# Keys prepared one pair earlier, and the division of x shared by two engines

## The chip, the cores and the metric

The kernel runs on one core of a Trainium2 chip. The metric is device time in microseconds, from one launch to its end. A core has five engines that matter here, each working through its own list of instructions in order: TensorE (PE: matrix products and transposes), VectorE (DVE), ScalarE (ACT), GpSimd (POOL), and SyncE (SP), which issues most of the DMA transfers. They wait for each other by semaphores only.

## The reference

The inputs pass through three stages. First attention without a score matrix, for 8 batches of 8 heads, 576 tokens and 64 dimensions:

```
q_s = exp(q - max over the 64 dimensions), divided by its sum (+1e-9)
k_s = exp(k - max over the 576 tokens),    divided by its sum (+1e-9)
kv  = k_s^T v            (64x64 for each head)
x   = q_s kv             (4608 tokens of 512 numbers, heads side by side)
```

Then a mixture of 8 experts: a gate picks for each token the expert with the largest logit (`x @ w_gate` plus a bias of the token's modality), and the token gets `gate * relu(x @ w1[e]) @ w2[e]`. Then a dense stage for all tokens: `a = x @ w1`, `b = x @ w2`, `out = (a * b) @ w3 @ w_out`.

## The kernel before, in words

**Order of the work.** The steps are not issued in the order of the source. Each is handed to `Plan.add` with its engine ("P" PE, "V" DVE, "S" ACT, "G" POOL, "D" a DMA on SP, "X" bookkeeping), an estimated cost in us, the keys that it reads and writes, and a `pri` that shifts its rank. `Plan.order` plays the list through with these costs: of the engines' next possible steps it takes the earliest, and among the steps that an engine could start within 0.02 us the one with the lowest rank. What comes out is the fixed order of instructions on each engine. The costs and the rank therefore decide only the order; the real times are the chip's. One such plan holds all of attention and the first part of the experts; it ends at a branch (L772), behind which a second plan holds the rest.

**Attention.** The 8 batches are taken as four pairs, `c` = 0 to 3, with `z = c % 2` choosing one of two buffers for keys, values and queries. For each pair there are these pieces:

- `load` (L246) issues the DMAs of q, k or v.
- `keys(c)` (L276): DVE takes maxima over the token blocks (L285 to L288), PE turns the result into PSUM bank 5 (L294), DVE finishes the maximum (L297), PE spreads it back to rows in bank 5 (L302), ACT copies it out (L305). Then, for four groups of heads, POOL subtracts it from the keys (L310; for the first pair DVE does) and ACT takes the exponential in place (L311).
- `kvs(c)` (L313): for each group of heads ACT copies the values beside a column of ones (L322), and PE multiplies keys by values in banks 4 and 5, 72 products a group (L329). DVE divides (L336 to L338), and a turn, a product with the gate weights and copies follow (L342 to L353). The result `bd` is what queries are multiplied with.
- `queries(n)` (L355): three tiles of queries at once get their row maximum subtracted on DVE (L364, L365). There are three such steps for a pair.
- `attend(c, j)` (L367), for nine tiles of 128 tokens, `j` = 0 to 8: PE turns the queries (L379), ACT takes the exponential (L382), PE multiplies with `bd` into a pair of PSUM banks `px` (L392), four heads of 73 columns in each bank: 64 of x, the sum, 8 of the gate. ACT copies the sums plus 1e-9 (L402) and the gate columns (L403), DVE takes the reciprocal (L404) and multiplies both banks by it into the x tile `xt` (L405). Two tiles together are stored to DRAM (L409).
- `route(c)` (L421) gives the pair's tokens their places in the experts' lists: some fifteen small DVE steps in a chain, PE products in bank 4 (L443, L445), and nine POOL scatters of 128 rows each (L416, `scatter`).

The main loop (L729 on) calls for pair `c`: the load of the keys of pair `c + 2`, `keys(c + 1)`, `route(c - 1)`, the nine `attend` with `queries` among them, the load of the queries, `kvs(c + 1)`, the load of the values. At `c = 2` it also makes the table of the first experts' work (`early_table`, L533), a chain of some thirty DVE instructions on single rows.

**Experts.** `slot` (L573) handles 512 or 256 tokens of one expert: SP reads the table (L571) and loads the order (L594) and the weights (L600), POOL gathers the tokens (L605), ACT scales them (L609). ACT and DVE split weights and tokens into a high and a low part (L586, L588, L629, L630), and PE multiplies (L642, L662). The first three slots draw on the tokens of pairs 0 and 1 alone, but their buffers take the place of attention's: `to_experts_a` (keys and values of even pairs) and `to_experts_b` (the rest, after all of attention; key `Mb`). The dense stage (L794 on) is nearly all PE.

Of the kernel before, what the change touches and what calls it, by code (L numbers as in the profile page):

```python
# [11 lines left out]
AF = mybir.ActivationFunctionType  # L12
ALU = mybir.AluOpType
# [5 lines left out]
B, H, S, D = 8, 8, 576, 64  # L19
NTOK = B * S  # L20
E = 8
NT = 9
# [94 lines left out]
def K(*a):  # L117
    return a


def vt_(n):
    return 0.065 + n * 0.00125
# [17 lines left out]
def body(tc, q, k, v, mod, wgate, mbias, w1, w2, m1, m2, w3, wo, out):  # L140
    nc = tc.nc
    V, G, SC, PE, SP = nc.vector, nc.gpsimd, nc.scalar, nc.tensor, nc.sync
# [133 lines left out]
    def keys(c):  # L276
# [18 lines left out]

        P.add("P", 0.9, over_partitions, r=[K("mx", z)], w=[K("bk", 5)])
        P.add("V", vt_(512), lambda: V.tensor_reduce(x_, bk.rearrange("p (c t) -> p c t", c=8), axis=AX.X, op=ALU.max), r=[K("bk", 5)], w=[K("cm", z)])  # L297
# [15 lines left out]
    def kvs(c):  # L313
# [6 lines left out]
        for g in range(4):  # L320
# [9 lines left out]

            P.add("P", 1.4, mm, r=[K("k", z, g), K("vp", g % 2)], w=[K("bk", 4), K("bk", 5)])
        for y in range(2):
# [34 lines left out]
    def attend(c, j):  # L367
# [12 lines left out]

        P.add("P", 0.9, tr, r=[K("qs", y)], w=[K("bk", qb)])
        P.add("S", ps_(512), lambda: SC.activation(T, pt, AF.Exp), r=[K("bk", qb)], w=[K("qT", n)])  # L382
# [10 lines left out]

        P.add("P", 0.8, mm, r=[K("qT", n)] + [K(x_, 2 * z + y) for x_ in ("bd", "bdg") for y in range(2)], w=pk)
        xb = (j // 2 + 5 * c) % 5
# [5 lines left out]
        by_bank = lambda t: t.rearrange("p (b g) e -> p b g e", b=2)  # L401
        P.add("S", 0.22, lambda: SC.activation(by_bank(r_.unsqueeze(2)), pv[:, :, :, 64:65], AF.Identity, bias=eps), r=pk, w=[qk])  # L402
        P.add("S", 0.22, lambda: SC.copy(by_bank(l_), pv[:, :, :, 65:73]), r=pk, w=[lk])  # L403
        P.add("V", 0.2, lambda: V.reciprocal(r_, r_), w=[qk])  # L404
        P.add("V", vt_(512), lambda: V.tensor_tensor(xdst, pv[:, :, :, 0:64], by_bank(r_.unsqueeze(2)).to_broadcast([128, 2, 4, 64]), op=ALU.mult), r=pk + [qk, lk], w=[rkey])  # L405
        if j % 2 or j == NT - 1:
            js = slice(j - j % 2, j + 1)
            dst = x_dram[128 * NT * c : 128 * NT * c + 128 * NT].rearrange("(p j) f -> p j f", j=NT)[:, js]
            P.add("D", 0.7 * (j % 2 + 1), lambda: SP.dma_start(dst, xt[xb][:, 0 : j % 2 + 1]), r=[K("xt", xb, i) for i in range(j % 2 + 1)], w=[K("x", c, j // 2)])  # L409

# [10 lines left out]
    def route(c):  # L421
# [34 lines left out]
        for t in range(NT):  # L456
            P.add("G", (1.04, 0.1), lambda t=t: scatter(pi[:, t : t + 1], tid[:, c, t]), r=[K("pi", z), K("gate", c), "order"], w=[K("scat", NT * c + t)], pri=-40)

# [268 lines left out]
    kvs(0)  # L727
    biases()
    for c in range(4):  # L729
        load("k", c + 2)  # L730
        keys(c + 1)
        if c:
            route(c - 1)
        if 2 * c == BEARLY:
            early_table()
        if c == 3:
            fa_keys = [k_ for k_ in P.last if isinstance(k_, tuple) and k_[0] in ("k", "v") and k_[1] == 0] + ["mods", K("mods", 0), K("mods", 1), K("bias", 1), "bs", "bsb", "mod", "modf", "zer"]
            P.add("X", 0.0, to_experts_a, w=fa_keys + ["Ma"])
        for j in range(NT):
            attend(c, j)  # L740
            if j % 3 == 2:
                queries(3 * c + j // 3 + 2)
        load("q", c + 2)
        kvs(c + 1)
        load("v", c + 2)
    fb_keys = [k_ for k_ in P.last if isinstance(k_, tuple) and (k_[0] in ("q", "qs", "qx", "qT", "bd", "bdg", "mx", "kr", "cm", "rk", "kT", "vp") or k_[0] in ("k", "v") and k_[1] == 1)]
# [222 lines left out]
```

## Time and profile before

| | us |
|---|---|
| median of 3 runs | 1305.44 (1302.25 to 1308.61) |
| the profiled execution | 1308.98, span 1307.3 |
| PE busy | 1210.3 (93%) |
| DVE busy | 642.1 (49%) |
| ACT busy | 450.9 (34%) |
| POOL busy | 282.6 (22%) |

The span is the time between the first and the last instruction of the profiled execution; 1.7 us of its time lie outside it. Busy shares are means over very different stages, so they have to be read for each stretch by itself. Times in the traces count from the span's start. "Idle before, releaser" tells how long an engine had stood idle before an instruction and which instruction let it go on; "issue" is waiting for which the profile shows no cause.

### The profile page before, as it was taken

What the parts mean: (1) busy time and instruction counts of PE and PEld (TensorE: products, weight loads), DVE (VectorE), ACT (ScalarE), POOL (GpSimd) and SP (SyncE); (2) the same over time, 40 slices, a digit from 0 to 9 for tenths busy, and PEclk for the clock granted to TensorE, in tenths of its full rate; (3) what the DMA queues carried; (4) which work ended last, traced back from release to release, by engine and by line L of the source; (5) the groups of instructions that cost most, each with busy time, mean ns of one, the idle gap of its engine ahead of it and who ended that gap; (6) DMA issues with size and microseconds to landing.
All of it is one profiled execution on the core that took longest, in us unless ns stands there. A gap on an engine that the chain in (4) does not pass through costs nothing.

```text
span 1307.3 us, 19789 instructions
## 1 busy us (share of the span) xinstructions
PE 1210.3 (93%) x8035; PEld 1014.1 (78%) x8035; DVE 642.1 (49%) x1092; ACT 450.9 (34%) x841; POOL 282.6 (22%) x262
## 2 busy tenths in 40 slices
PE   4777578999999999999999999999999999999996
PEld 3556457878788888999887888888888888888885
DVE  6988577896278777998642303030303030212120
ACT  3543364444354544465542212121212121212120
POOL 0454426543034233543100010101010101010101
PEclk9886778999999999999999999999999999999998
DMA  9962255756345583684540010101010101010000
GB/s 356 393 254 59 73 220 139 248 197 206 131 130 167 196 278 109 214 302 130 204 144 33 13 53 6 59 2 63 1 65 1 65 1 65 1 65 1 33 1 33
DMA packets 67960, 153.94 MB, mean 118 GB/s; under 512 B 11758, under 2 KB 14354, under 8 KB 67858
## 3 DMA queue, kind: packets, MB, share of 16 engines
q1 hardware_dynamic: 60786, 133.13, 29.4%
q0 software_dynamic: 7072, 19.44, 4.6%
q8 instruction: 65, 1.06, 0.4%
q14 instruction: 37, 0.30, 0.1%
HBM read 129.67 MB, written 39.70 MB: 130 GB/s over the span
## 4 chain that ended last, share of the span: by engine, by line
PE 67%; DVE 4%; issue 1%; DMA 0%; ACT 0%; POOLq 0%; DVEq 0%; ACTq 0%
PE pb L906 30%; PE pb L925 15%; PE pb L662 10%; PE pb L642 7%; PE pb L854 3%; DVE w2l L588 1%; PE pb L625 1%; DVE hTl L647 1%; PE pb L841 0%; DVE w1l L588 0%; DVE xt L683 0%; DVE xt L682 0%; DVE xt L687 0%; DVE xt L685 0%; DVE xt L688 0%
## 5 line engine op out<-in xcount | busy, mean ns | idle before, releaser
L913 DVE TENSOR_TENSOR xg<-xg,pb 128x512 f32<-128x512 f32 x72 | 49.5, 688 | 411.3 <-PE pb L906 406.0
L933 POOL DMA_INDIRECT out_dram<-misc,oall x36 | 34.9, 969 | 634.7 <-ACT misc L931 634.7
L642 PE MATMUL pb<-xTh,w1h 128*128 128x512 f32 (+1 forms) x384 | 135.3, 352 | 7.4 <-DVE hTl L647 7.3
L662 PE MATMUL pb<-hTh,w2h 128*128 128x512 f32 (+1 forms) x384 | 134.5, 350 | 0.0
L662 PE MATMUL pb<-hTl,w2h 128*128 128x512 f32 (+1 forms) x384 | 133.1, 347 | 1.4 <-DVE hTl L647 1.3
L642 PE MATMUL pb<-xTl,w1h 128*128 128x512 f32 (+1 forms) x384 | 134.1, 349 | 0.0
L642 PE MATMUL pb<-xTh,w1l 128*128 128x512 f32 (+1 forms) x384 | 133.8, 348 | 0.0
L662 PE MATMUL pb<-hTh,w2l 128*128 128x512 f32 (+1 forms) x384 | 132.8, 346 | 0.0
L826 ACT CAST pTh<-xg 128x512 fp32r<-128x512 f32 x76 | 47.1, 622 | 197.4 <-DVE xg L913 197.4
L925 PE MATMUL pb<-w2l,pTh 128*128 128x512 f32 x288 | 114.9, 399 | 0.0
L925 PE MATMUL pb<-w2h,pTh 128*128 128x512 f32 x288 | 113.5, 394 | 0.0
L925 PE MATMUL pb<-w2h,pTl 128*128 128x512 f32 x288 | 112.9, 392 | 0.0
L906 PE MATMUL pb<-xTh,hTh 128*128 128x512 f32 x288 | 112.3, 390 | 0.0
L906 PE MATMUL pb<-xTl,hTh 128*128 128x512 f32 x288 | 112.2, 390 | 0.0
L906 PE MATMUL pb<-xTh,w1l 128*128 128x512 f32 x288 | 112.1, 389 | 0.0
L906 PE MATMUL pb<-xTh,w1h 128*128 128x512 f32 x288 | 112.0, 389 | 0.0
L906 PE MATMUL pb<-xTl,w1h 128*128 128x512 f32 x288 | 112.0, 389 | 0.0
L906 PE MATMUL pb<-xTh,hTl 128*128 128x512 f32 x288 | 112.0, 389 | 0.0
L642 PEld LDWEIGHTS pb<-xTh,w1h 128*128 128x128 f32 x384 | 73.6, 192 | 17.8 <-DVE hTl L647 8.6
L646 ACT ACTIVATE hTh<-pb 128x512 fp32r<-128x512 f32 (+1 forms) x96 | 48.6, 509 | 107.2 <-PE pb L642 106.5
L662 PEld LDWEIGHTS pb<-hTl,w2h 128*128 128x128 f32 x384 | 73.1, 190 | 10.2 <-DVE hTl L647 1.8
L642 PEld LDWEIGHTS pb<-xTl,w1h 128*128 128x128 f32 x384 | 73.7, 192 | 9.3 <-issue 0.5
(255 smaller groups left out, 2370.4 us busy)
## 6 DMA issues: line engine op xcount, KB each, us to landing
w1r<-in_moe_w_dram SPq DMA_DIRECT2D x12, 2048.0 KB
w2r<-in_moe_w_dram SPq DMA_DIRECT2D x12, 2048.0 KB
xt<-in_moe_w_dram SPq DMA_DIRECT2D x32, 512.0 KB
kt<-in_k_dram SPq DMA_DIRECT2D x8, 1152.0 KB
qt<-in_q_dram SPq DMA_DIRECT2D x8, 1152.0 KB
vt<-in_v_dram SPq DMA_DIRECT2D x8, 1152.0 KB
yo<-yT SPq DMA_DIRECT2D x9, 1024.0 KB
x_dram<-xt SPq DMA_DIRECT2D x16, 512.0 KB
```

The source lines that it names most:

```text
L588: P.add(g, c, lambda: e.tensor_tensor(lo(), raw(), hi().bitcast(F32), op=ALU.subtract), r=[K(nm + "r", i), K(nm + "h", i), extra], w=[K(nm ...
L625: PE.transpose(p[:, kk, 128 * t : 128 * t + 128], xg[h][:, t, c : c + 128], ident)
L642: PE.matmul(p(), lhsT=W1(i)[:, TURN[kk], ms], rhs=XT(z)[:, kk, cols], start=(kk == 0 and c == 0), stop=(kk == 3 and c == 2))
L646: P.add("S", ps_(N), lambda hh=hh, p=p: SC.activation(hh(), p(), AF.Relu), r=[K("bk", pb), "Mb"], w=[K("hh", h, m) for h in hs])
L647: P.add("V", vt_(N), lambda hh=hh, hl=hl, p=p: V.scalar_tensor_tensor(out=hl(), in0=p(), scalar=0.0, in1=hh().bitcast(F32), op0=ALU.max, o ...
L662: PE.matmul(p(), lhsT=W2(i)[:, f, ns], rhs=HT(y)[:, f, cols], start=(f == 0 and c == 0), stop=(f == 7 and c == 2))
L826: P.add("S", (ps_ if psum else sb_)(n), lambda: SC.copy(hi(), src), r=sk, w=[hk])
L854: PE.matmul(bank[pb], lhsT=th[i][:, 8 * p2 + g], rhs=PT(y)[:, g], start=(g == 0 and n == 0), stop=(g == 7 and n == 2))
L906: PE.matmul(dst, lhsT=mat[i][:, kk, ms], rhs=XT[z][:, kk], start=(c == 0), stop=(c == 11))
L913: P.add("V", vt_(512), lambda a_=a_, p_=p_, p2=p2: V.tensor_tensor(p_, a_, bank[p2], op=ALU.mult), r=[K("bk", p2), K("a", wb), K("ring", 1 ...
L925: PE.matmul(bank[pb], lhsT=PT(i)[:, f, ts], rhs=WP[y][:, f], start=(c == 0), stop=(c == 23))
L933: P.add("G", (1.04, 0.74), lambda o3=o3, c=c: G.indirect_dma_start(out=out, out_offset=bass.IndirectOffsetOnAxis(ap=oall[:, c : c + 1], ax ...
```

## The change

- `keys` is called a pair earlier: `keys(1)` ahead of the loop, and `keys(c + 2)` behind the sixth tile of pair `c` in place of `keys(c + 1)` ahead of the first.
- `kvs(c + 1)` and the load of the next queries stand behind the third tile, no longer behind the ninth; the load of the values stands beside that of the keys.
- The division of x: DVE multiplies bank 0 only (four heads, 128x256), and ACT multiplies bank 1 in four instructions, one for each head, with the reciprocal as the scale for each partition. The store waits for both halves.
- The scatters of `route` get a rank 160 higher, and a cost of 1.4 in place of 1.04.
- `to_experts_a` is called at `c = 2`, no longer at `c = 3`.
- Some of the planner's costs are larger (0.9 to 1.0, 1.4 to 1.9, 0.8 to 1.05, 0.22 to 0.28).

```diff
-        P.add("P", 0.9, over_partitions, r=[K("mx", z)], w=[K("bk", 5)])
+        P.add("P", 1.0, over_partitions, r=[K("mx", z)], w=[K("bk", 5)])
...
-            P.add("P", 1.4, mm, r=[K("k", z, g), K("vp", g % 2)], w=[K("bk", 4), K("bk", 5)])
+            P.add("P", 1.9, mm, r=[K("k", z, g), K("vp", g % 2)], w=[K("bk", 4), K("bk", 5)])
...
-        P.add("P", 0.9, tr, r=[K("qs", y)], w=[K("bk", qb)])
+        P.add("P", 1.0, tr, r=[K("qs", y)], w=[K("bk", qb)])
...
-        P.add("P", 0.8, mm, r=[K("qT", n)] + [K(x_, 2 * z + y) for x_ in ("bd", "bdg") for y in range(2)], w=pk)
+        P.add("P", 1.05, mm, r=[K("qT", n)] + [K(x_, 2 * z + y) for x_ in ("bd", "bdg") for y in range(2)], w=pk)
...
-        P.add("S", 0.22, lambda: SC.activation(by_bank(r_.unsqueeze(2)), pv[:, :, :, 64:65], AF.Identity, bias=eps), r=pk, w=[qk])
+        P.add("S", 0.28, lambda: SC.activation(by_bank(r_.unsqueeze(2)), pv[:, :, :, 64:65], AF.Identity, bias=eps), r=pk, w=[qk])
...
-        P.add("V", vt_(512), lambda: V.tensor_tensor(xdst, pv[:, :, :, 0:64], by_bank(r_.unsqueeze(2)).to_broadcast([128, 2, 4, 64]), op=ALU.mult), r=pk + [qk, lk], w=[rkey])
+        P.add("V", vt_(256), lambda: V.tensor_tensor(xdst[:, 0], pv[:, 0, :, 0:64], r_[:, 0:4].unsqueeze(2).to_broadcast([128, 4, 64]), op=ALU.mult), r=pk[:1] + [qk, lk], w=[rkey + (0,)])
+
+        def second():
+            for h in range(4):
+                SC.activation(xdst[:, 1, h], pv[:, 1, h, 0:64], AF.Copy, scale=r_[:, 4 + h : 5 + h])
+
+        P.add("S", 0.8, second, r=pk[1:] + [qk, lk], w=[rkey + (1,)])
...
-            P.add("G", (1.04, 0.1), lambda t=t: scatter(pi[:, t : t + 1], tid[:, c, t]), r=[K("pi", z), K("gate", c), "order"], w=[K("scat", NT * c + t)], pri=-40)
+            P.add("G", (1.4, 0.1), lambda t=t: scatter(pi[:, t : t + 1], tid[:, c, t]), r=[K("pi", z), K("gate", c), "order"], w=[K("scat", NT * c + t)], pri=120)
...
+    keys(1)
     for c in range(4):
         load("k", c + 2)
-        keys(c + 1)
+        load("v", c + 2)
         if c:
             route(c - 1)
         if 2 * c == BEARLY:
             early_table()
-        if c == 3:
             fa_keys = [k_ for k_ in P.last if isinstance(k_, tuple) and k_[0] in ("k", "v") and k_[1] == 0] + ["mods", K("mods", 0), K("mods", 1), K("bias", 1), "bs", "bsb", "mod", "modf", "zer"]
             P.add("X", 0.0, to_experts_a, w=fa_keys + ["Ma"])
         for j in range(NT):
             attend(c, j)
             if j % 3 == 2:
                 queries(3 * c + j // 3 + 2)
-        load("q", c + 2)
-        kvs(c + 1)
-        load("v", c + 2)
+            if j == 2:
+                load("q", c + 2)
+                kvs(c + 1)
+            if j == 5:
+                keys(c + 2)
```

## Rows read from the trace of the kernel before

**Rows 1.** Page, the chain that ended last, shares of the span

```profile
PE 67%; DVE 4%; issue 1%; DMA 0%; ACT 0%; POOLq 0%; DVEq 0%; ACTq 0%
```

**Rows 2.** Busy time of each engine in stretches, from 35.6 to 500 us

```profile
core 0: us, PE busy (x) PEld busy (x) DVE busy (x) ACT busy (x) POOL busy (x), PEclk, DMA share, GB/s
...
35.60:61.20 25.60, 17.05 (x490) 14.01 (x490) 25.50 (x33) 15.56 (x33) 14.39 (x4) 0.86 1.05 391
...
72.50:99.70 27.20, 20.17 (x514) 16.55 (x515) 24.22 (x40) 13.35 (x33) 19.38 (x15) 0.85 0.57 202
99.70:113.60 13.90, 10.85 (x196) 8.59 (x188) 10.10 (x23) 6.01 (x11) 4.39 (x7) 0.62 0.37 58
113.60:147.40 33.80, 23.28 (x487) 18.73 (x486) 21.67 (x49) 11.93 (x30) 20.55 (x22) 0.67 0.17 49
147.40:163.90 16.50, 8.39 (x210) 6.95 (x210) 12.02 (x43) 4.73 (x10) 4.64 (x5) 0.77 0.43 122
163.90:176.10 12.20, 11.16 (x296) 9.18 (x296) 6.78 (x16) 6.29 (x24) 0.00 (x0) 0.75 1.03 396
...
226.00:361.00 135.00, 128.75 (x592) 106.24 (x591) 91.07 (x192) 54.99 (x96) 48.34 (x47) 1.00 0.59 193
361.00:500.00 139.00, 139.00 (x634) 115.56 (x634) 107.75 (x165) 64.71 (x114) 51.11 (x40) 0.99 0.56 190
```

**Rows 3.** Timeline of ACT: the last instruction ahead of pairs 2 and 3

```profile
112.29 0.19 ACT L353 COPY bd<-pb 128x32 f32<-128x32 f32 x1 [0.66 <-PE pb L350]
...
163.72 0.19 ACT L353 COPY bd<-pb 128x32 f32<-128x32 f32 x1 [2.79 <-remote]
```

**Rows 4.** Timeline of POOL: the subtractions, and the first scatter

```profile
78.41 5.23 POOL L310 TENSOR_TENSOR kt<-kt,kr 128x1152 f32<-128x1152 f32 x2 [19.73 <-ACT kr L305]
84.59 2.36 POOL L416 DMA_INDIRECT order_dram<-tid,pi  x1 [0.95 <-DVE xt L405]
...
90.79 5.21 POOL L310 TENSOR_TENSOR kt<-kt,kr 128x1152 f32<-128x1152 f32 x2
...
137.04 5.22 POOL L310 TENSOR_TENSOR kt<-kt,kr 128x1152 f32<-128x1152 f32 x2
```

**Rows 5.** Timeline of PE: first and last piece of one group of L329

```profile
126.91 1.01 PE L329 MATMUL pb<-vp,kt 64*64 64x65 f32 x19
...
138.50 0.60 PE L329 MATMUL pb<-vp,kt 64*64 64x65 f32 x10 [1.03 <-issue]
```

**Rows 6.** Groups by line, 72.5 to 176.1 us

```profile
L405 DVE TENSOR_TENSOR xt<-pp,rq 128x512 f32<-128x512 f32 x26 | 17.8, 687 | 2.0 <-DVE rq L404 0.4 <-PE pb L379 0.4 <-DVE t_tadb L500 0.2
...
L403 ACT COPY l<-pp 128x64 f32<-128x64 f32 x26 | 5.4, 206 | 0.0
```

**Rows 7.** Groups by line, 0 to 215 us

```profile
L586 ACT CAST w1h<-w1r 128x512 fp32r<-128x512 f32 x13 | 7.3, 619 | 1.2 <-PE pb L642 1.1
...
L609 ACT ACTIVATE xg<-xg,ord 128x512 f32<-128x512 f32 x6 | 4.2, 722 | 9.6 <-DMA xg<-x_dram,ord 9.6
...
L338 DVE TENSOR_TENSOR bd<-pb,rk 128x256 f32<-128x256 f32 x8 | 3.1, 420 | 0.0
```

**Rows 8.** Timeline of ACT: a small copy and the next instruction

```profile
45.51 0.20 ACT L403 COPY l<-pp 128x64 f32<-128x64 f32 x1
45.60 0.61 ACT L382 ACTIVATE qT<-pb 128x512 f32<-128x512 f32 x1
```

**Rows 9.** Timeline of DVE: a long subtraction, start and end of the table

```profile
92.17 5.45 DVE L365 TENSOR_TENSOR qs<-qt,qx 128x1536 f32<-128x1536 f32 x1
...
120.36 0.12 DVE L449 TENSOR_TENSOR cnt<-cnt,pb 128x8 f32<-128x8 f32 x1
...
153.29 0.15 DVE L530 TENSOR_SCALAR tab<-t_tad 1x3 int32<-1x3 f32 x1
```

**Rows 10.** Timeline of SP: order of the first slots

```profile
154.46 4.11 SPq L594 DMA_DIRECT2D ord<-order_dram  x3
```

**Rows 11.** Busy time in a stretch of 5 us, columns as in rows 2

```profile
175.00:180.00 5.00, 1.07 (x33) 0.76 (x33) 4.45 (x10) 4.29 (x11) 1.11 (x2) 1.00 0.66 263
```

More of the change, by code (lines that the diff above doesn't have):

```diff
@@ L408, in attend @@
             dst = x_dram[128 * NT * c : 128 * NT * c + 128 * NT].rearrange("(p j) f -> p j f", j=NT)[:, js]
-            P.add("D", 0.7 * (j % 2 + 1), lambda: SP.dma_start(dst, xt[xb][:, 0 : j % 2 + 1]), r=[K("xt", xb, i) for i in range(j % 2 + 1)], w=[K("x", c, j // 2)])
+            P.add("D", 0.7 * (j % 2 + 1), lambda: SP.dma_start(dst, xt[xb][:, 0 : j % 2 + 1]), r=[K("xt", xb, i, a) for i in range(j % 2 + 1) for a in range(2)], w=[K("x", c, j // 2)])
     scattered = [False]
```

## The prediction

> **What bounds the kernel.** I read the chain of waits first: PE makes 67% of the span [rows 1], and all that the chain shows lies behind the branch at 361 us. There PE is busy without a gap for the first 139 us [rows 2]. The change touches nothing there, so it can only move the branch. Ahead of it, from 226 us on, PE is busy 128.75 of 135 us [rows 2]: the slots of the first experts, untouched too. What is left is attention and the start of slot 0. So the question is how much earlier slot 0 can begin; a microsecond gained there should reach the end almost whole.
>
> Then I read busy times by stretches cut where a pair of batches begins and ends [rows 2]. The reader is to see three kinds of stretch. In pair 0 (35.6 to 61.2) DVE is busy 25.50 of 25.60 us: DVE is the bound. In pairs 1 and 2 (72.5 to 99.7 and 113.6 to 147.4) PE is busy for 74% and 69% of the stretch at a granted clock of 0.85 and 0.67, and DVE for 89% and 64%. And there are two gaps in which no tile of x is made at all: 99.7 to 113.6 and 147.4 to 163.9, together 30.4 us. They end when the last gate copy of the next pair's `bd` is done, at 112.29 and 163.72 [rows 3]. So the keys and the key-value product of the next pair are late. POOL's timeline says why: it subtracts for two groups of heads at 78.41, then turns to the scatters of the previous pair at 84.59, and subtracts for the other groups only at 90.79; for the next pair the second half waits until 137.04 [rows 4]. Pair 3 (163.9 to 176.1), for which all was prepared, takes 12.2 us for its nine tiles with PE busy 91%.
>
> **The change, part by part.** *Keys and kvs earlier.* No instruction is added or removed: each `keys` still issues its DVE maxima, PE turns, four POOL subtractions and five ACT steps, and its loads on SP. They get a better rank. Ahead of pair 1, which starts at 72.5, I expect nothing: `keys(1)` keeps its place in front of the first tile, and DVE is full in pair 0. For pair 2, `keys(2)` must still wait for bank 5 until `kvs(1)` is done, just ahead of pair 1, so its first subtraction stays near 78.4. But the scatters now rank behind, so the four subtractions run in two times 5.2 us, to about 89 instead of 96.0. From the last subtraction to `bd` it took 112.3 - 96.0 = 16.3 us [rows 3, 4], with scatters running; at most that again puts `bd` at 105, and without what the scatters cost PE (below) near 97. Pair 1 ends at 99.7, so of its gap of 13.9 us at most 5.6 are left. The same holds a pair later, where the last subtraction ended at 142.3 [rows 4] behind nine scatters. Both gaps can close or nearly so.
>
> They do not give back their whole 30.4 us, because work was done in them: DVE 10.10 + 12.02 us, PE 10.85 + 8.39 us [rows 2]. So I add up loads from 72.5 to 176.1, five stretches, 103.6 us:
>
> PE: 20.17 + 10.85 + 23.28 + 8.39 + 11.16 = 73.85 us, unchanged.
> DVE: 24.22 + 10.10 + 21.67 + 12.02 + 6.78 = 74.79 us.
> ACT: 13.35 + 6.01 + 11.93 + 4.73 + 6.29 = 42.31 us.
>
> *The division.* DVE's 128x512 multiply took 687 ns [rows 6]; a multiply of 128x256 from PSUM of the same kind took 420 ns [rows 7]. That saves 0.267 us a tile, 7.2 us for 27 tiles: DVE falls to 67.6 us. For ACT the trace has no such instruction. A copy of 128x64 from PSUM took 206 ns [rows 6]; a scale from a register per partition costs about 0.10 us, the difference of 722 and 619 ns for 128x512 [rows 7]. So I estimate 0.31 us each and 1.2 us a tile if the four run one after another, the upper bound. Neighbours on ACT overlap: L403 begins at 45.51 and takes 0.20, and the next instruction begins at 45.60, 0.11 us before that end [rows 8]. I take 0.2 us each, 0.8 us a tile, 21.6 us for 27 tiles; the lower bound, without any cost for the scale, is 0.4 us a tile. ACT rises to 63.9 us (53 to 75). It is still below PE. The Trainium skill, page "ScalarE: Activation LUTs", section "What ACT_TABLE_LOAD costs", gives 186 ns plus 0.833 ns an element, 93 ns more for a pointer operand and an overlap of 93 ns; an estimate from that is 239 ns each and 0.96 us a tile, and ACT would stand at 68.1 us. The same page's rules for authors would leave a multiply on VectorE, which speaks against this edit; no row here shows that instruction.
>
> *Head of the queue.* ACT now waits for a DVE result within a tile. Behind the four multiplies stand the exponentials of the next queries, and PE waits for these. The wait is short if DVE reaches the reciprocal promptly, and up to one DVE subtraction if not; one took 5.45 us while POOL subtracted [rows 4, 9].
>
> *The rest at nothing.* The planner's costs issue no instruction. The values' load moves past the queries' on SP, in a time when SP's loads are behind the 391 GB/s of the DMA engines anyway [rows 2]. If that cover were gone, a late load would hold `kvs(1)`, a few us. The release of the even pool only moves an order. The later scatters must be done before slot 0 reads its order: two times nine at the 1.4 us that the planner now assumes, on a POOL that has spare time in pair 2.
>
> *The sum.* From 72.5 on, PE has the most to do, 73.9 us. In the best stretch it was busy 91%, in pair 1, which has everything to do side by side, 74% [rows 2]. That bounds the new length: 81.2 us (end of attention at 153.7), or 99.8 us (172.3). I take the middle, 85%, since the gaps go but ACT's new wait and the shorter slack remain: 86.9 us, an end at 159.4 instead of 176.1. The gain is 16.7 us, with ends of 3.8 and 22.4. Pair 0 may add up to 9 times 0.267 = 2.4 us; I count nothing, as `kvs(1)` waits for POOL there. From the profiled 1308.98 that gives 1292.3. That execution is 3.5 us above the median of the runs, so for the median I take 1305.44 - 16.7 = 1288.7, rounded to 1289.
>
> **The rivals.** *Slot 0 is not ready.* Its table is finished by DVE at 153.29, SP issues the order at 154.46 [rows 9, 10], and weights and gathered tokens then keep the DMA engines full from 163.9 to 176.1 (a share of 1.03 [rows 2]), which falls to 0.66 in 175 to 180 [rows 11]: about 23 us from table to data. The data came just when attention ended. If the table ends at T, slot 0 starts no earlier than about T + 23. The chain of its thirty small steps ran from 120.36 to 153.29 [rows 9], 33 us. If pair 1 ends as before and the chain still takes 30 us, T is about 148, and the gain 5 us: 1300. For it speaks that each small step waits behind a long DVE one, against it that PE's long product of the next paragraph fell into this chain.
>
> *The scatters hold PE again.* One group of L329, 72 products, took from 126.91 to 139.1 instead of some 2 us, in pieces with "issue" between them [rows 5], while POOL scattered ahead of its subtraction at 137.04 [rows 4]. Bank 4 ties `kvs(c + 1)` to `route(c - 1)`, and the scatters follow the same `route`. If this grows by the same 10 us in pair 2 the gain is 7 us: 1299.
>
> *Slower.* ACT stands at the head of its queue for the reciprocal. With a mean wait of w a tile ACT needs 42.3 + 21.6 + 27w us. It costs more than 0.5% once this passes 103.6 + 6.5, which is w above 1.71 us, the length of an undisturbed query step on DVE. With w = 2.2 us it is 123.3 us, 19.7 us more than before: 1325. DVE is the busier engine, which speaks for some wait; that the planner puts other ACT work ahead speaks against so much.
>
> *More gained.* If denser work gets PE its full clock (it had 0.62 to 0.85 here, and 1.00 later [rows 2]), PE's 73.9 us shrink to about 55, and DVE's 67.6 us are the bound; at 91% that is 74 us, a gain of 29: 1276.
>
> **How the numbers follow.** A measurement of this kernel can tell about 0.5%, 6.5 us, from no change: faster is below 1298.9, slower above 1312. Forecast (gain 9 to 23): 0.50. More gained: 0.15. Slot 0 or the scatters, or nothing shown at all: 0.21, of which 0.03 still below 1298.9. Slower: 0.14. So faster 0.68, same 0.18, slower 0.14. The range takes in the forecast and most of the cases on both sides: 1274 to 1305; the likeliest case's own is 1282 to 1297.
>
> **What would show it.** The end of the last tile near 159 instead of 176.1; the pauses before pairs 2 and 3 gone; all four L310 of a pair ahead of the scatters; DVE's multiply near 420 ns; four ACT multiplies of 0.3 us; PE full from slot 0 on some 17 us earlier. The prediction is wrong if ACT shows long waits on L404, if the table stays near 150, or if the branch comes no earlier though attention ends earlier.

## The result, and the profile after

The changed kernel takes 1323.05 us (1322.72 to 1324.29) where the kernel before, on the same chip, takes 1307.03 us (1302.25 to 1309.39): a ratio of 1.012 [1.0098, 1.0143], some 16 us slower. Forecast were 1289 us and a gain of 16.7.

All of it lies ahead of the branch. I read four marks from PE's timeline and the chain of waits: the first product of x of each pair, the end of the last one, the first product of slot 0, and the branch. Behind the branch every kernel of this study takes 945 to 948 us, so these marks carry the whole difference.

| us from the start | pair 1 | pair 2 | pair 3 | attention ends | slot 0 | branch |
|---|---|---|---|---|---|---|
| before | 72.5 | 113.6 | 161.7 | 176.0 | 187.1 | 360.8 |
| after | 72.0 | 117.8 | 166.2 | 187.2 | 199.4 | 374.1 |

Each pair has 288 products of x, 32 a tile, and the marks go by this count. Before, eight products of pair 3 ran at 161.7 and the others from 164.0 on, where [rows 2] begin the pair.

Busy times of the changed kernel between these marks, columns as in [rows 2]:

```profile
72.00:117.80 45.80, 32.77 (x699) 27.44 (x698) 33.53 (x56) 25.55 (x76) 22.62 (x21) 0.67 0.35 126
117.80:166.20 48.40, 27.82 (x672) 23.11 (x670) 27.91 (x78) 23.53 (x74) 23.48 (x24) 0.72 0.17 52
166.20:187.30 21.10, 15.72 (x327) 12.30 (x327) 10.07 (x33) 14.24 (x58) 3.66 (x6) 0.76 0.99 356
```

The reader is to see two things. The gaps of [rows 2] are no longer there: pairs follow each other. And yet pairs 2 and 3 start 4 us later than before, and pair 3 takes 21.0 us instead of 12.2 (14.3 with its first eight products). The gaps have moved into the pairs: PE makes no product of x from 90.9 to 106.5 and from 135.4 to 150.2, together 30.4 us again. The loads came nearly as forecast: PE 32.77 + 27.82 + 15.72 = 76.3 us (forecast 73.9), DVE 71.5 (67.6), ACT 63.3 (63.9). But they are spread over 115.3 us, so PE is busy 66% and not 85%.

The groups of the two halves of the division, from 72 to 187.3 us, answer to [rows 6]:

```profile
L409 ACT ACTIVATE xt<-pp,rq 128x64 f32<-128x64 f32 x100 | 23.2, 316 | 19.5 <-DVE rq L404 13.3 <-DVE xt L405 6.1
...
L405 DVE TENSOR_TENSOR xt<-pp,rq 128x256 f32<-128x256 f32 x26 | 11.0, 422 | 7.4 <-ACT xt L409 3.4 <-ACT l L403 1.7 <-PE pb L379 1.0
```

The durations are those of the forecast too (420 ns; 0.31 us each before overlap). New are the waits: ACT stands 19.5 us for DVE, in part for DVE's multiply L405 and not only for its reciprocal, and DVE stands 3.4 us for ACT's multiplies. The two halves run one after the other: in none of the 36 tiles do they overlap, and ACT's half comes first in 18. In the built program, whichever half is issued second waits for the first, since both read the one PSUM tile of the pair.

The last tiles of pair 3 show what that does, since DVE has nothing else left to do there. ACT's timeline:

```profile
183.79 0.30 ACT L402 ACTIVATE rq<-pp,eps 128x8 f32<-128x8 f32 x1
183.94 0.25 ACT L403 COPY l<-pp 128x64 f32<-128x64 f32 x1
184.99 0.93 ACT L409 ACTIVATE xt<-pp,rq 128x64 f32<-128x64 f32 x4 [0.81 <-DVE xt L405]
185.79 0.61 ACT L382 ACTIVATE qT<-pb 128x512 f32<-128x512 f32 x1
186.27 0.30 ACT L402 ACTIVATE rq<-pp,eps 128x8 f32<-128x8 f32 x1
```

and PE's:

```profile
183.98 0.74 PE L392 MATMUL pp<-bd,qT 64*64 64x73 f32 x32 [0.32 <-ACT qT L382]
186.46 0.74 PE L392 MATMUL pp<-bd,qT 64*64 64x73 f32 x32 [1.74 <-ACT qT L382]
```

A tile takes 2.48 us, from L402 at 183.79 to L402 at 186.27; the two ahead of it took 2.49 and 2.41. The exponential L382 that PE needs for the next tile stands behind the four multiplies, and these behind DVE. Before, nine tiles took 12.2 us, 1.36 us each (1.38 from one L402 to the next).

The second loss is in the product of keys and values. POOL's first scatter, and PE under the scatters:

```profile
77.07 11.97 POOL L310 TENSOR_TENSOR kt<-kt,kr 128x1152 f32<-128x1152 f32 x4 [21.87 <-ACT kr L305]
90.73 1.23 POOL L422 DMA_INDIRECT order_dram<-tid,pi  x1 [1.69 <-DVE pi L458]
```

```profile
89.61 1.25 PE L392 MATMUL pp<-bd,qT 64*64 64x73 f32 x32 [0.40 <-DVE pf L457]
...
94.95 1.95 PE L329 MATMUL pb<-vp,kt 64*64 64x65 f32 x44
97.11 0.41 PE L329 MATMUL pb<-vp,kt 64*64 64x65 f32 x3 [0.21 <-issue]
97.87 0.27 PE L329 MATMUL pb<-vp,kt 64*64 64x65 f32 x1 [0.34 <-issue]
...
103.56 0.36 PE L329 MATMUL pb<-vp,kt 64*64 64x65 f32 x1 [0.23 <-issue]
104.27 2.56 PE L329 MATMUL pb<-vp,kt 64*64 64x65 f32 x83 [0.35 <-issue]
106.53 0.38 PE L392 MATMUL pp<-bd,qT 64*64 64x73 f32 x2
```

The four subtractions run in a row ahead of the scatters, as forecast. The product then falls on the nine scatters, and for seven microseconds PE gets one to three matmuls every 0.72 us and waits for nothing the profile names. The product of pair 2 stretches from 87.0 to 106.9, that of pair 3 from 135.1 to 155.4: the stall of [rows 5] in both pairs instead of one. So `bd` is hardly earlier than in [rows 3]:

```profile
113.47 0.23 ACT L353 COPY bd<-pb 128x32 f32<-128x32 f32 x1
...
161.83 0.29 ACT L353 COPY bd<-pb 128x32 f32<-128x32 f32 x2
```

### The profile page after: what moved, and what is told of

Its sections match the earlier page's. It is cut to its first block, busy times and chain, and to the rows that moved or that the text cites. A ratio compares the mean times of both kernels' runs of the same rounds, so it can differ in the third digit from the quotient of the medians.

```text
span 1321.3 us, 19925 instructions
## 1 busy us (share of the span) xinstructions
PE 1212.8 (92%) x8035; PEld 1016.2 (77%) x8035; DVE 638.4 (48%) x1092; ACT 479.7 (36%) x985; POOL 282.2 (21%) x262
## 4 chain that ended last, share of the span: by engine, by line
PE 66%; DVE 3%; issue 1%; ACT 0%; DMA 0%; POOLq 0%; ACTq 0%; DVEq 0%
PE pb L914 30%; PE pb L933 15%; PE pb L668 10%; PE pb L648 7%; PE pb L862 3%; DVE w2l L594 1%; PE pb L631 1%; DVE hTl L653 1%; PE pb L849 0%; DVE w1l L594 0%; DVE xt L689 0%; DVE xt L688 0%; DVE xt L693 0%; DVE xt L691 0%; DMA out_dram<-misc,oall 0%
## 5 line engine op out<-in xcount | busy, mean ns | idle before, releaser
L648 PEld LDWEIGHTS pb<-xTh,w1h 128*128 128x128 f32 x384 | 73.8, 192 | 16.7 <-DVE hTl L653 7.5
L648 PEld LDWEIGHTS pb<-xTl,w1h 128*128 128x128 f32 x384 | 73.9, 192 | 10.0 <-DVE xTl L636 1.2
L668 PEld LDWEIGHTS pb<-hTl,w2h 128*128 128x128 f32 x384 | 73.3, 191 | 10.3 <-DVE hTl L653 1.8
```

The lines of the kernel that those rows point to most:

```text
L648: PE.matmul(p(), lhsT=W1(i)[:, TURN[kk], ms], rhs=XT(z)[:, kk, cols], start=(kk == 0 and c == 0), stop=(kk == 3 and c == 2))
L668: PE.matmul(p(), lhsT=W2(i)[:, f, ns], rhs=HT(y)[:, f, cols], start=(f == 0 and c == 0), stop=(f == 7 and c == 2))
```

## The experiments

The first theory, A, was that the shared division costs; the rival, B, that earlier keys put the product on the scatters and the subtractions on DVE's operations. Ratios are to the kernel before on the same chip, and the chips differ: the kernel before takes 1307.0 us where the changed kernel ran, 1310.0 where e1 to e4 did, 1302.7 for e5 to e8, 1302.9 for e9 to e12, 1309.7 for e13 to e15 and 1308.6 for e16 to e18. Where ratios from different chips are set against each other, both intervals count, together some 0.25%, and the difference of the chips besides, of which more below. With the kernel before run once more (e15) attention's end, slot 0 and the branch came within 1 us of the first trace; these two executions took 1308.6 and 1309.0 us, and no trace shows the kernel before where it takes 1302.7.

**Halves of the change.** The changed kernel with one multiply on DVE (e1), the kernel before with the shared division alone (e2), and the changed kernel with the PSUM pair as two tiles (e3):

```diff
 e1
-V.tensor_tensor(xdst[:, 0], pv[:, 0, :, 0:64], ...)   # 128x256
-P.add("S", 0.8, second, ...)                          # four 128x64
+V.tensor_tensor(xdst, pv[:, :, :, 0:64], ...)         # 128x512
 e3
-pairs = [pair_pool.tile([128, 2, 512], F32, ...) for i in range(2)]
+pairs = [[pair_pool.tile([128, 512], F32, ...) for a in range(2)] for i in range(2)]
```

> The changed kernel with the division undone: DVE multiplies both banks of a tile in one instruction again, keys stay a pair ahead. Theory A (the division costs the time: the two halves wait for each other, and ScalarE waits at the head of its queue): pair 3 takes about 12 us for its nine tiles again instead of 21, the time is 1308 to 1314 us. Theory B (the earlier keys cost the time: the product of keys and values falls on the scatters, and four subtractions in a row hold VectorE): pair 3 is shorter, but pairs 1 and 2 stay as long, 1317 to 1325 us.

> The kernel before with the division shared between the two engines, and nothing else. Theory A: each tile of pair 3 takes about 2.4 us instead of 1.4, and 1314 to 1320 us in all. Theory B: within 3 us of before, 1304 to 1310.

> The changed kernel with the pair of PSUM banks as two tiles of one bank each, so that the two halves of the division need not wait for each other; the copies of the sums and of the gate columns become two instructions each, two more small ScalarE instructions in all for each kind of copy. Theory A with the mutual wait as its main part: 1310 to 1317 us, waits between the two multiplies gone. Theory A with ScalarE's wait for the reciprocal, or its load, as the main part: 1320 to 1328. Theory B: 1320 to 1326.

Measured: e1 1316.73 us, 1.0048 [1.0032, 1.0064]; e2 1320.93 us, 1.0076 [1.0056, 1.0097]; e3 1323.55 us, 1.0099 [1.0079, 1.0119]. Both halves cost: 0.76% for the division, 0.48% for preparing ahead. They do so in different places. In e2 attention ends at 191.1 us, 15 us later than before, and the branch comes as much later as in the changed kernel but for 1.6 us. In e1 attention ends at 175.5, where it ended before (176.0), though pair 3 takes 17.4 us and not the 12 that theory A expected; its time is just below theory B's range. What e1 loses it loses between slot 0 and the branch, above all in one wait of PE. It goes back to DVE, which ahead of that waits for POOL:

```profile
221.73 1.48 DVE L687 TENSOR_SCALAR xt<-xt 128x512 int32<-128x512 int32 x1 [5.40 <-POOL xt L686]
...
225.79 1.12 PE L625 MATMUL pb<-ident,xg 128*128 128x128 f32 x4 [7.62 <-DVE xTl L630]
```

One plan holds attention and the first slots, so preparing ahead changes the order there too; in the changed kernel, whose slots begin 11 us later, PE waits only 1.9 us for the same split of tokens. Splitting the tile (e3) takes the wait of one half for the other away: they overlap in 22 of 36 tiles, a tile of pair 3 takes 1.71 us where tiles follow each other, and slot 0 begins 3.8 us earlier than in the changed kernel. It adds two small ACT instructions a tile, and PE then waits 10.4 us for POOL in the slots; by its time it cannot be told from the changed kernel.

**The scatters.** Three kernels without the scatters of pairs 0 and 1: the changed one (e4), the one before (e5), and e1 (e7).

```diff
-lambda t=t: scatter(pi[:, t : t + 1], tid[:, c, t])
+lambda t=t: scatter(pi[:, t : t + 1], tid[:, c, t]) if c > 1 else None
```

> The changed kernel without the scatters of pairs 0 and 1 (18 on GpSimd; the experts' order of these tokens is left out, so the first slots gather row 0, with as many bytes). The order of all else is the same. Theory B: the pauses of TensorE inside the product of keys and values go (some 20 us between 97 and 148), the time falls to 1300 to 1310. Theory A: the pauses hide behind other waits, 1317 to 1323.

> The kernel before without the 18 scatters of the order of pairs 0 and 1 (that part of the computation is left out). Without the same scatters the changed kernel gained some 18 to 20 us. Theory S (the scatters hold PE's product of keys and values, and the change only made this dearer by putting the product on top of them): the kernel before loses less by them, 5 to 12 us, so 1298 to 1305. Theory N (the scatters cost both kernels the same, the change has nothing to do with it): 1288 to 1292.

> The changed kernel with the division whole on DVE, without the 18 scatters of pairs 0 and 1 (left out of the computation). To be read against the kernel before without the same scatters, in this call. Theory S (preparing ahead is sound and only the scatters eat its gain): 10 to 17 us below that kernel. Theory H (the pair's work is bound elsewhere, by DVE operations held while POOL subtracts): within 4 us of it.

Measured: e4 1302.56 us, 0.9936 [0.9916, 0.9956]; e5 1293.23 us, 0.9926 [0.9909, 0.9942]; e7 1292.64 us, 0.9918 [0.9901, 0.9935]. The scatters cost the kernel before 0.74% (9.5 us, on the chip of e5, which is within theory S's 5 to 12 though the time is in neither range) and the changed one 1.84%. e4's time is in theory B's range. In e4 the products of pairs 2 and 3 take 11.9 and 7.8 us instead of 19.9 and 20.2; in e5 that of pair 3 takes two times about 5 us. The two prices come from chips on which the stall differs, as shown below, so their difference is not all the change's. On the chip of e5 alone the price is 0.74% for the kernel before and 1.32% with preparing ahead (1.005 of e6, below, to 0.9918): there theory S is right that preparing ahead makes the scatters dearer. Where S failed: without scatters, preparing ahead gains nothing (e7 and e5, same chip). Its attention does end earlier, at 155.1 against 159.2 us, but PE then waits 7.7 us in the slots as in e1, scatters or not:

```profile
202.35 1.12 PE L625 MATMUL pb<-ident,xg 128*128 128x128 f32 x4 [7.67 <-DVE xTl L630]
```

Busy times from the start of pair 1 to the end of attention, in e5 and in e7:

```profile
72.40:159.20 86.80, 61.33 (x1686) 51.67 (x1682) 75.37 (x168) 41.83 (x104) 26.86 (x12) 0.80 0.47 161
67.50:155.10 87.60, 58.94 (x1687) 50.19 (x1686) 75.14 (x168) 42.59 (x104) 27.85 (x12) 0.83 0.50 177
```

DVE, the third column, is busy 87% in e5 and 86% in e7, PE 71 and 67%. Once PE does not stall, DVE is the busiest engine in either order.

**The rank of the scatters** put back in e1 (e6):

```diff
-P.add("G", (1.4, 0.1), ..., pri=120)
+P.add("G", (1.04, 0.1), ..., pri=-40)
```

> The changed kernel with the division whole on DVE, and the scatters at the rank and cost that they had before (so the keys, the product and their loads ahead stay). Theory S (late scatters fall into the product and ahead of the gathers of slot 1, which opened 7.6 us on PE): at the old rank the scatters go back between the subtractions, slot 1 gets its gathers in time, and 1305 to 1311 is left. Theory H (what costs is the subtractions' hold on DVE and PE's product beside attention, whatever the scatters' rank): no better than 1316.7, 1314 to 1322.

Measured: 1309.05 us, 1.005 [1.0033, 1.0067], the ratio of e1. Its attention ends at 163.4 us where e1's ends at 175.5, and the product of pair 2 takes 7.1 us instead of 17. That is not the rank's work: up to the product of pair 3 every engine does the same steps in the same order in e1 and e6, and they ran on different chips. What the rank changes lies behind attention. PE in slot 1:

```profile
201.58 0.48 PE L625 MATMUL pb<-ident,xg 128*128 128x128 f32 x1 [10.11 <-ACT xg L609]
```

and POOL ahead of it:

```profile
187.24 0.98 POOL L416 DMA_INDIRECT order_dram<-tid,pi  x1 [5.92 <-DMA order<-order_dram]
...
191.14 1.15 POOL L416 DMA_INDIRECT order_dram<-tid,pi  x1
192.59 1.51 POOL L605 DMA_INDIRECT xg<-x_dram,ord  x1 [0.30 <-issue]
```

The gathers of slot 1 stand behind the nine scatters of pair 2, and these wait twice for reads of the order (5.2 and 5.9 us). The gathers end 24.7 us behind slot 0's first product (22.5 before), and PE has run out of slot 0 after 18.3. Slot 0 to branch is 184.7 us here, 173.7 before. So the old rank does not bring slot 1 its gathers in time, as theory S had it; by the ratio theory H holds.

**The subtractions on DVE**, in e1 (e8), in e1 without the scatters (e10), in the kernel before (e11), in the changed kernel (e12), and in e8 with the old rank (e14):

```diff
-en, e_, c_ = ("G", G, gt_(1152)) if c else ("V", V, vt_(1152))
+en, e_, c_ = "V", V, vt_(1152)
```

> The changed kernel with the division whole on DVE and the subtractions of the keys of pairs 1 to 3 on DVE instead of POOL: 12 at about 1.35 us, 16 us more for DVE, and no POOL subtraction that could hold a DVE operation. Theory H (some 16 us of DVE time are lost in holds while POOL subtracts, and the keys come late by POOL's 12 us a pair): the work costs DVE nothing net and the keys come earlier, 1305 to 1313. Theory S (holds are hidden, the scatters are what counts): DVE has 16 us more in attention, most of it on the path, 1322 to 1332.

> The changed kernel with the division whole on DVE and all subtractions on DVE, without the 18 scatters of pairs 0 and 1 (left out of the computation). With the subtractions on POOL the same scatters cost a ratio of 0.013 (1.0048 against 0.9918). Theory I (scatters and subtractions hurt together: both want POOL, and the product falls on the scatters because the subtractions come late): without the subtractions the scatters cost less, 0.002 to 0.006, so 0.9875 to 0.9915. Theory J (the scatters slow PE's product by themselves, wherever the subtractions run): 0.009 to 0.013, so 0.980 to 0.9845.

> The kernel before with the subtractions of pairs 1 to 3 on DVE, nothing prepared ahead. With them on DVE and prepared ahead it was 0.9934. Theory H (POOL's subtractions were the late part and the hold on DVE; once they are gone most of the gain is there without preparing ahead): 0.990 to 0.998. Theory P (preparing ahead is what pays, and the subtractions only hid it): DVE has 16 us more and the product is as late as before, 1.000 to 1.008.

> The changed kernel whole, shared division too, with the subtractions on DVE. The shared division cost 0.0076 alone and 0.0072 on top of preparing ahead (1.012 against 1.0048). Theory R (round trip, independent of DVE's load): again 0.006 to 0.009 on top of 0.9934, so 0.9995 to 1.0025. Theory L (the shared division pays where DVE is the busier engine, which it now is with 16 us more): below 0.9934, 0.987 to 0.9935.

> Division whole on DVE, subtractions on DVE, prepared ahead, and the scatters at their old rank and cost. At the new rank it was 0.9934. Theory Q (the rank matters only through POOL's queue, which now holds no subtraction): 0.991 to 0.9955. Theory E (earlier scatters feed the table and slot 1 earlier): 0.985 to 0.991.

Measured: e8 1294.58 us, 0.9934 [0.9917, 0.995]; e10 1284.91 us, 0.9864 [0.9847, 0.9882]; e11 1298.91 us, 0.9963 [0.9948, 0.9978]; e12 1304.69 us, 1.0018 [1.0008, 1.0027]; e14 1309.85 us, 1.0008 [0.9992, 1.0024]. Theory H held in e11: 16 us more of DVE work cost nothing net, and the kernel is 0.37% faster. e8 lies below both of its ranges; it ran on a chip on which PE stalls less, see below. Against e1, on a chip like its own, e14 is 0.40% faster. In the changed kernel DVE's operations were held while POOL subtracted from 77.07 to 89.04 (the third has 1.71 us of its own, the others 0.16 to 0.23 us):

```profile
78.69 1.11 DVE L442 SCALAR_TENSOR_TENSOR eq<-lg,c 128x72 f32<-128x72 f32 x1
...
80.00 2.32 DVE L460 TENSOR_SCALAR s<-s 128x9 f32<-128x9 f32 x1
...
82.49 4.05 DVE L365 TENSOR_TENSOR qs<-qt,qx 128x1536 f32<-128x1536 f32 x1
...
86.80 2.33 DVE L456 TENSOR_TENSOR pos<-pos,oh 128x72 f32<-128x72 f32 x1
```

In e8 the twelve L365 take 1744 ns in the mean, against 2141 in the changed kernel. The Trainium skill, page "SBUF — State Buffer", section "Who interferes with whom", says that a VectorE instruction with two SBUF inputs contends with a GpSimd instruction that reads SBUF, and that whoever issues first keeps the shared ports while the other blocks wholly; the rows agree for L365 and L456. L460, with one input, was held too.

The shared division costs the same 0.8% with DVE that much busier (e12 over e8): theory L is out. Against e8, e10 lies between its theories: the scatters cost 0.70%. e14 misses both of its ranges; it is 0.74% slower than e8, and the next experiment shows that this is not the rank's work.

**The same order on two chips.** In e8 and e14 every engine does the same steps in the same order through all of attention; the first difference is on POOL, at 184.8 us in e8. Between 86 and 89.8 us they are alike to 0.1 us, scatters included. PE in e14:

```profile
90.03 0.64 PE L329 MATMUL pb<-vp,kt 64*64 64x65 f32 x27 [0.37 <-issue]
90.96 0.35 PE L329 MATMUL pb<-vp,kt 64*64 64x65 f32 x5 [0.29 <-issue]
91.68 0.35 PE L329 MATMUL pb<-vp,kt 64*64 64x65 f32 x5 [0.37 <-issue]
...
102.12 1.50 PE L329 MATMUL pb<-vp,kt 64*64 64x65 f32 x44 [0.94 <-issue]
```

and in e8:

```profile
87.24 2.36 PE L329 MATMUL pb<-vp,kt 64*64 64x65 f32 x144
89.80 1.27 PE L329 MATMUL pb<-vp,kt 64*64 64x65 f32 x69 [0.19 <-ACT vp L322]
91.36 1.32 PE L329 MATMUL pb<-vp,kt 64*64 64x65 f32 x74 [0.29 <-issue]
```

The same product takes 16.5 us in one and 5.5 us in the other, and attention ends at 171.5 and 157.6 us. The DMA queues of e14 (packets, MB, share of 16 engines) in two stretches of 2 us, 88 to 90 ahead of the scatters' packets and 96 to 98 among them:

```profile
q8 instruction: 1, 0.02, 3.6%
...
q8 instruction: 1, 0.02, 6.5%
```

In e8 it was 3.0% at 88 to 90 and 10.3% at 92 to 94. A packet of the instruction queue takes 1.8 times as long among the scatters in e14 and 3.4 times in e8, whose PE pauses behind this product, between 93.3 and 97.3. But from 90.4 to 96.0 us, where e14's PE paused five times, that queue moved no packet at all. To see whether the place in PE's instruction stream matters, e8, e14 and the changed kernel got 64 small matmuls ahead of everything, with the rest in the same order (e16, e17, e18):

```diff
-setup()
+setup(), [PE.matmul(pairs[0][:, 0, 0:8], lhsT=ident, rhs=ident[:, 0:8], start=True, stop=True) for _ in range(64)]
```

> Preparing ahead, division whole and subtractions on DVE, scatters at the new rank (0.9934), with 64 small matmuls of 128x8 ahead of everything on PE, in its idle time at the start; every other instruction in the same order. Theory F (PE's pauses under the scatters hang on where its instruction fetch falls): the time moves by 4 us or more, so outside 0.990 to 0.9965. Theory G (they hang on the order of work alone): the time stays, 0.991 to 0.996.

> The same with the scatters at their old rank (1.0008), and the same 64 matmuls ahead. Theory F: the product of pair 2 no longer takes 16.5 us at the same place, and the time moves by 4 us or more, most likely down, below 0.9975. Theory G: 0.999 to 1.003.

> The changed kernel itself with the same 64 matmuls ahead (1.012 [1.0098, 1.0143] without). Theory F: it moves by 4 us or more either way, outside 1.009 to 1.015. Theory G: 1.009 to 1.015.

Measured: 1.0093 [1.0076, 1.011], 1.0115 [1.0096, 1.0133], 1.0213 [1.0192, 1.0233]. The experiment has a flaw of mine, in the PE timeline of e16:

```profile
1.45 27.47 PE L718 MATMUL pp<-ident 128*128 128x8 f32 x128 [1.45 <-POOL ident masks.py:199]
```

They took 27.5 us, not the idle time, and pair 0 starts at 51.6 us instead of 36.5. So the times say nothing on the place in the stream. They do say something on the rank. e16 and e17 ran on one chip, again with the same order through attention; the product of pair 2 takes 17.2 and 17.3 us, attention ends at 185.8 and 185.5, and the ratios differ by 0.2%, within their intervals. So the rank is not what sets e8 apart from e14. The place in PE's stream cannot be it either, since PE's steps up to there are the same. What does go with the stall is the chip. The kernels with keys ahead and scatters, ordered by the time of the kernel before on their chip:

| ran on the chip of | kernel before, us | product of pair 2 and of pair 3, us |
|---|---|---|
| e5 to e8 | 1302.7 | e6 7.1 and 13.9; e8 5.5 and 12.1 |
| e9 to e12 | 1302.9 | e12 6.9 and 11.0 |
| the changed kernel | 1307.0 | 19.9 and 20.2 |
| e16 to e18 | 1308.6 | e16 17.2 and 18.3; e17 17.3 and 18.4; e18 20.2 and 20.1 |
| e13 to e15 | 1309.7 | e14 16.5 and 18.2 |
| e1 to e4 | 1310.0 | e1 17.0 and 20.6; e3 19.0 and 20.0 |

None with a long product is on the first two chips, none with a short one on the others. There is one trace for each kernel, and no kernel with keys ahead and scatters ran on chips of both kinds, so that the chip decides is not shown by itself, nor what in it does. But it is the nearest account of e1 against e6 and of e8 against e14. e8's 0.9934 is the best time of a complete kernel here, and I would not count on it; e14's 1.0008 is the same order of work in attention on a chip of the other kind.

**How the shared division costs.** e2 with ScalarE taking two heads (e9), and with ScalarE multiplying by a constant column (e13); e15 is the kernel before once more.

```diff
 e9
-V 128x256 of bank 0; SC.activation of 4 heads of bank 1
+V 128x384, three heads of each bank; SC.activation of the fourth head of each bank
 e13
-scale=r_[:, 4 + h : 5 + h]
+scale=eps
```

> The kernel before with the division shared, but ScalarE takes two of the eight heads of a tile instead of four (VectorE multiplies 128x384, ScalarE twice 128x64). Four heads alone cost a ratio of 1.0076 to the kernel before. Theory R (what costs is the round trip: ScalarE at the head of its queue for VectorE's result, and one engine behind the other on the same PSUM tile; it is paid whatever ScalarE's share): 1.005 to 1.009. Theory Q (what costs is the number of ScalarE multiplies, some 0.2 us each): half of it, 1.001 to 1.0045.

> The kernel before with the shared division, in which ScalarE multiplies its half by a constant column instead of the reciprocals (that half of x is not divided: part of the computation is left out). ScalarE's four multiplies no longer wait for VectorE; their number, their PSUM tile and the order of the two halves on it stay. With the wait it was 1.0076 [1.0056, 1.0097]. Theory W (the wait at the head of ScalarE's queue costs): 0.999 to 1.003. Theory C (what costs is the longer chain until a PSUM pair is free, the two halves one after the other): 1.005 to 1.009.

> The kernel before once more, unchanged, for a trace from the chip on which the other two run: a ratio of 0.998 to 1.002, the attention's end and the branch within 5 us of 176.0 and 360.8. If the marks of one kernel move by more than that, differences of single marks between traces say little.

Measured: e9 1312.11 us, 1.0066 [1.0048, 1.0084]; e13 1317.81 us, 1.0063 [1.0045, 1.0081]; e15 1308.81 us, 0.9997 [0.9984, 1.001]. Theory W falls: without the wait for the reciprocal ACT's idle time ahead of its multiplies goes from 20.3 us (e2) to 6.0 us, and nearly all of the cost stays. The number is in theory C's range. The group of the multiplies in e13, from pair 1 on:

```profile
L409 ACT ACTIVATE xt<-pp,eps 128x64 f32<-128x64 f32 x104 | 24.5, 333 | 6.0 <-DVE xt L405 5.4 <-issue 0.5
```

Tiles of pair 3 on ACT, in e2:

```profile
183.89 0.29 ACT L402 ACTIVATE rq<-pp,eps 128x8 f32<-128x8 f32 x1
...
185.02 0.93 ACT L409 ACTIVATE xt<-pp,rq 128x64 f32<-128x64 f32 x4 [0.24 <-DVE xt L405]
185.82 0.29 ACT L402 ACTIVATE rq<-pp,eps 128x8 f32<-128x8 f32 x1
```

in e9:

```profile
163.55 0.28 ACT L402 ACTIVATE rq<-pp,eps 128x8 f32<-128x8 f32 x1
...
164.86 0.52 ACT L409 ACTIVATE xt<-pp,rq 128x64 f32<-128x64 f32 x2 [0.44 <-DVE xt L405]
165.27 0.28 ACT L402 ACTIVATE rq<-pp,eps 128x8 f32<-128x8 f32 x1
```

and in e13:

```profile
181.02 0.93 ACT L409 ACTIVATE xt<-pp,eps 128x64 f32<-128x64 f32 x4 [0.24 <-DVE xt L405]
...
183.02 0.93 ACT L409 ACTIVATE xt<-pp,eps 128x64 f32<-128x64 f32 x4 [0.18 <-issue]
```

Tiles in a row take turns of two lengths: 1.93 and 1.99 us in e2, 1.92 and 2.00 in e13, 1.65 and 1.72 in e9, against 1.38 in the mean before. ACT is idle for only 0.2 to 0.4 us of a tile: where tiles follow each other, its own steps and the one wait for DVE's L405 set the pace, and the wait for the reciprocal adds nothing. With two multiplies instead of four a tile adds 0.31 us instead of 0.58, about half, as theory Q has it. e9's time does not show this: attention ends at 170.2 us, and PE waits 10.65 us for the gathers at slot 1, as in e6. So by the times R and Q are not decided.

## Why the prediction was wrong

*The bound.* Right that only the branch can move, and that a loss passes through: attention +11.2 us, slot 0 +12.3, branch +13.3.

*Keys ahead.* Right in place: the four subtractions run ahead of the scatters and both gaps are closed. Wrong in what follows from it: `bd` of pair 2 was to be ready between 97 and 105 us and came at 113.7 (112.5 before), since the product took 20 us under the scatters, and the gaps opened again inside the pairs. Nothing is gained by it in time, with scatters (e1) or without (e7); what it costs by itself is a wait of 7.6 us in the slots, on which the prediction has no word.

*The loads.* Right: DVE's multiply 422 ns, four ACT multiplies 0.93 us from end to end and 0.8 in effect, PE 76.3, DVE 71.5 and ACT 63.3 us.

*The sum.* This is the step that failed: "85%, since the gaps go but ACT's new wait and the shorter slack remain". The loads of a whole stretch were to pack around PE; they took 115.3 us instead of 86.9, with PE busy 66%. (The middle of 91 and 74% would have been 82.5%, and the gain 14 us.) Shown in its place are two limits that a sum of loads does not hold. Tiles in a row go at the pace of one tile's own chain through ACT and DVE (2.48 us; 1.38 before), though ACT has spare time on the average; with the division undone attention ends where it did before (e1). And the product falls on the scatters in both pairs (20 us each, 8 to 12 without), which eats what the earlier keys should give. Where no scatters run, DVE is the busiest engine (e5, e7), not PE.

*The rule weighed.* The Trainium skill, page "ScalarE: Activation LUTs", section "Rules for kernel authors", leaves a multiply to VectorE. The runs agree in sign: the shared division alone costs 0.76%.

*The rivals.* "The scatters hold PE again" is what happened, in both pairs. Whether 10 us was the right price is open: the scatters cost the changed kernel 20 us (e4), but what they cost the kernel before was measured only on a chip where they stall PE less (e5). "Slower" has the sign and nearly the time, by another way: ACT's wait was 0.75 us a tile (19.5 over 26), not the 1.71 it needed, and without most of it the loss remains (e13). That 1325 is so near to 1323 is luck. What it says of the exponentials behind the multiplies is there: PE's product waits 11.4 us for L382. "Slot 0 is not ready" did not occur; slot 1 was not, in e6 and e9. "More gained" needed a denser PE, which did not come.

*Left open.* By the marks the division makes nearly the whole loss (branch at 374.1 us with both, 372.6 with the division alone), while by the ratios it makes 0.76 of 1.2%; they ran on different chips. Without scatters the shared division costs 0.18% by the ratios of e4 and e7, but 10 us by their times and 14 us by the end of attention (168.9 and 155.1); these two ran on chips of the two kinds. How PE's pauses come about, and why some chips have fewer, was not shown.

## What to carry to other kernels

Loads added up over a stretch bound its length from below and say little about it: follow one tile through every engine, write down what each waits for, and compare that with its pace where tiles stand alone. Before a step is moved earlier, look at what will then run beside it, and at who stands next in line once it is done: here the freed time went to a product under the scatters, and to a wait of PE behind attention that the new order brought. A gain of half a per cent should be tried on a second chip before it is believed, and a difference between two runs put down to an edit only where the edit changes the order of work ahead of it.

## What the hardware showed

PE, with nothing to wait for, got one to five matmuls each 0.72 us while POOL's scatters of 128 rows ran, on and off for some 11 us (e14). In the same order of work on another chip (e8) the same product ran at full pace beside the first of these scatters, and PE paused for 2.7 us only in the product of x behind it. The Trainium skill, page "Runtime: NRT & Kernel Launch", section "Instruction fetch mechanics", says that instructions are fetched in blocks of 16 KiB by a DMA queue and that crossing a block is mostly hidden; the packets of 0.02 MB in the instruction queue agree. That the pauses are late fetches is not shown: e8 paused while a packet of 3.3 us was under way, but e14 paused five times between 90.4 and 96.0 us with none.

Two engines that read different banks of one PSUM tile did not overlap here (in none of 36 tiles): the waits of the built program put them in order. With a tile for each bank they overlapped in 22 of 36, for up to 0.43 us (e3).
